# Splitting the next pair's keys ahead of a normalization, and another order of three products, in a fused attention and MLP kernel

## The chip, the cores and the metric

The kernel runs on one core of one Trainium2 chip. The time is the device time of one execution, in microseconds (us). Before the change it is 675.01 us, the median of three runs (674.80 to 675.87).

The engines by their names in the profile: PE is TensorE (matmuls) and PEld its loading of the stationary operand, DVE is VectorE, ACT is ScalarE, POOL is GpSimd, SP is SyncE, which here only issues DMAs. Each engine works through its own queue in order.

## The reference

Attention with a band of 96 keys and 8 global keys, then a two-layer MLP with a gate; 4 batches, 8 heads, 768 positions, 64 columns per head, 512 model columns, 2048 hidden ones. All is float32.

```python
scores = q @ k.T / sqrt(64) - slope[h] * dist       # where kept, else -1e9
a = exp(scores - max); a = a / (sum(a) + 1e-9)
x = (a @ v).reshape(3072, 512)
h = x @ w_in                                        # 512 -> 2048
g = h * clip(h + 3, 0, 6) / 6
out = g @ w_out                                     # 2048 -> 512
```

## The kernel before

**Numbers.** TensorE multiplies in a reduced float32 form (fp32r). To keep full precision each operand is split into a high and a low part, and a product is made of three: high times high, high times low, low times high. The parts of the hidden activation g are gh (made by GpSimd in the layers' part, L183, by ScalarE before it, L185) and gl = g - gh (VectorE, L190). The weights are w1h, w1l, w2h and w2l, decoded from their words while blocks 0 and 1 run (w2l by VectorE at L399). In the later attention queries are split into q1 (ScalarE, L751) and q2 (VectorE, L755), and keys into kx: the high part in one half of the partitions (GpSimd, L752), the low part in the other (VectorE, L758).

**Blocks and pairs.** The work is eight blocks of 384 positions (four batches, two halves each). Attention goes by pairs of heads, four pairs to a block, 32 pairs in all, numbered through. Pairs 0 to 11 (blocks 0 to 2) are done first, with plain float32 keys, beside the first halves of the MLP. Then comes *the layers' part*: while the MLP of block i runs (i from 2 on), the attention of block i + 1 is done beside it. So pairs 12 to 15 (block 3) are done beside the MLP of block 2, and pairs 16 to 31 beside the MLPs of blocks 3 to 6. Block 7's MLP runs alone.

**The MLP of a block.** It loops over f, 16 slices of 128 hidden columns. `first` (L159) makes hp, the hidden slice, with 12 matmuls of 384 columns. `gate` (L170) makes g on ScalarE and VectorE. gh and gl follow, and `second` (L193) adds the slice to three accumulators (three tiles tt of 128 positions) with nine matmuls of 512 columns, three per tile. `halves` (L438) puts `first` of f ahead of `second` of f - 1, so that the gate's chain runs beside TensorE's work. It yields after each `first` with its gate and after each `second`.

**Attention beside it.** `attention` (L586) fills a list of units for a block, six to a pair, and at each yield one unit's steps are put into the engines' queues. For a pair `me` and the next one, `after`, a pair's six units hold:

- units 0 to 2: `scores(t)` (L763), for each tile t of 128 queries four matmuls on kx with q1 and q2 (L778), the distances and the row minimum on VectorE (L785), the exponentials and their sums on ScalarE (L789);
- unit 3: `sum_up` (L793: add and reciprocal, L797 and L798), `normalize(0)` and `normalize(1)` (two multiplications each on GpSimd, L807), then `after.split(0)`: q1 and the high keys;
- unit 4: `normalize(2)`, `spread(0)`, and `after.split(1)`: q2;
- unit 5: `spread(1)`, `spread(2)`, `fetch`, and `after.split(2)`: the low keys, then the load of a pair further on.

`spread` (L822) transposes 32 x 32 blocks on VectorE (L832) and stores them to memory (L834); `fetch` (L837) reads them back as *weights* of the values (L841) with four DMAs. `values` (L850) multiplies them with v (L859). It is called for two pairs at once, in the sixth unit of every second pair. For pairs 12 to 15 all units come one place later, behind an empty one.

**What sets the order.** PE, GpSimd and SP keep the order of the program text as it runs (`in_order`, L576). VectorE and ScalarE are ordered by the framework's scheduler, which estimates times. So a step that is moved in a unit moves on GpSimd exactly so, and on VectorE as the scheduler sees fit. g has one buffer, gh, gl and hp two, the blocks that `spread` fills two.

Of the kernel before, what the change touches and what calls it, by code (L numbers as in the profile page):

```python
# [20 lines left out]
NT = 3  # L21
# [36 lines left out]
class Kernel:  # L58
# [134 lines left out]
    def second(self, f, acc, gh, gl):  # L193
        for tt in range(NT):
            tk = slice(tt * P, (tt + 1) * P)
            for j, (a, w) in enumerate(((gh, self.w2h), (gl, self.w2h), (gh, self.w2l))):
                self.nc.tensor.matmul(acc[tt], lhsT=a[:, tk], rhs=self.w2(w, f),  # L197
                                      start=(f == 0 and j == 0), stop=(f == NF - 1 and j == 2))

# [386 lines left out]
    def attention(self, i, x, first):  # L586

        units = [[] for _ in range(2 * NF - 2)]
        pairs = [first or Pair(self, i * NPAIR, x, False)]
        pairs[0].x = x  # L590
        if first is None:
            for k in range(3):
                pairs[0].split(k, False)
            units[1].append(lambda: self.load_next(pairs[0].n, False))
        for p in range(NPAIR):
            n = i * NPAIR + p
            me, after = pairs[p], Pair(self, n + 1, x, False) if n + 1 < len(self.blocks) * NPAIR else None
            pairs.append(after)
            at = units[6 * p:]
            for t in range(NT):  # L600
                at[t].append(lambda t=t, me=me: me.scores(t))
            at[3] += [me.sum_up, lambda me=me: me.normalize(0), lambda me=me: me.normalize(1)]
            at[4] += [lambda me=me: me.normalize(2), lambda me=me: me.spread(0)]
            at[5] += [lambda me=me: me.spread(1), lambda me=me: me.spread(2), me.fetch]
            for t in range(NT if after else 0):
                at[t + 3].append(lambda t=t, after=after: after.split(t))
            if p % 2 == 1:
                at[11] += [lambda me=pairs[p - 1]: me.values("x"), lambda me=me: me.values("s")]
        return units, pairs[NPAIR]
# [327 lines left out]
```

## Time and profile before

| What | us |
|---|---|
| median of three runs | 675.01 |
| the profiled execution | 674.91 |
| its span, first to last instruction | 673.0 |
| PE busy | 657.1 |
| VectorE busy | 438.6 |
| ScalarE busy | 282.9 |
| GpSimd busy | 192.6 |

The span is what the profile's rows lie in; 1.9 us of the execution lie around it. The granted TensorE clock is 0.998 of full speed. A row of a timeline gives the start in us from the span's start, how long the group took, engine and line, the operation, what it writes and reads, how many there are in the group, and in brackets how long the engine had stood idle before it and what ended that. Matmuls overlap, so a row's duration on PE is longer than the step from one matmul to the next: the steps are read from the starts. A row of the waits gives the total, the number of times and the longest.

### The profile page before, as it was taken

Reading aid. Unit: us, or ns where it says so; the run is one execution under the profiler, and the core shown is the slowest. Engines: PE = TensorE matmul, PEld = TensorE weight load, DVE = VectorE, ACT = ScalarE, POOL = GpSimd, SP = SyncE. Lnnn points to the kernel's source line nnn. Section 1 sums busy time; section 2 is a strip of 40 time slices with the busy share of each in tenths; the row PEclk is TensorE's granted clock in tenths of the full one; section 3 lists DMA queues with packets and bytes.
Section 4 is the critical chain, followed back from the end, with each engine's and each line's share of the span. In section 5 each row is a group of like instructions: output and inputs, shape, how many; then the busy total and the mean of one; then the engine's idle time right before and its main releaser. Section 6 shows DMA issues by size and latency. Waiting matters only on the chain.

```text
span 673.0 us, 11339 instructions
## 1 busy us (share of the span) xinstructions
PE 657.1 (98%) x3913; PEld 590.5 (88%) x3913; DVE 438.6 (65%) x1186; ACT 282.9 (42%) x744; POOL 192.6 (29%) x354
## 2 busy tenths in 40 slices
PE   7999899999999999999999999999999999999996
PEld 6788789999999889899989999899989999989995
DVE  8799899999975666457653676447762676422221
ACT  6899655554446333144333433143331443231111
POOL 2855400000000443233340343315431343302110
PEclk9999999999999999999999999999999999999999
DMA  8677432333303446524654367534555255510001
GB/s 255 176 230 242 146 124 100 121 110 110 97 29 133 131 135 181 158 94 132 165 140 119 103 172 189 147 94 126 138 160 141 79 150 142 141 47 2 1 1 52
DMA packets 62611, 84.33 MB, mean 125 GB/s; under 512 B 8784, under 2 KB 48720, under 8 KB 62544
## 3 DMA queue, kind: packets, MB, share of 16 engines
q1 hardware_dynamic: 62256, 83.25, 43.1%
q8 instruction: 33, 0.54, 0.3%
q14 instruction: 34, 0.28, 0.1%
q10 hardware_dynamic: 288, 0.26, 0.1%
HBM read 62.52 MB, written 20.97 MB: 124 GB/s over the span
## 4 chain that ended last, share of the span: by engine, by line
PE 84%; DMA 5%; ACT 4%; DVE 3%; issue 1%; POOL 1%; SPq 0%; POOLq 0%; ACTq 0%
PE hp L165 38%; PE acc L197 32%; DMA wst<-w 5%; ACT n L789 2%; PE sp L778 2%; PE xp L859 2%; PE tp L859 2%; PE sp L197 2%; PE tp L197 2%; PE xp L197 2%; PE tp L778 2%; POOL n L807 1%; ACT pt L819 1%; DVE n L785 1%; ACT wz L370 0%
## 5 line engine op out<-in xcount | busy, mean ns | idle before, releaser
L176 ACT ACTIVATE g<-hp,small 128x384 f32<-128x384 f32 x127 | 73.9, 582 | 256.0 <-PE hp L165 226.1
L165 PE MATMUL hp<-xh,w1h 128*128 128x384 f32 x512 | 174.0, 340 | 0.0
L165 PE MATMUL hp<-xh,w1l 128*128 128x384 f32 x512 | 172.8, 337 | 0.0
L165 PE MATMUL hp<-xl,w1h 128*128 128x384 f32 x512 | 171.9, 336 | 0.0
L183 POOL TENSOR_SCALAR gh<-g 128x384 fp32r<-128x384 f32 x96 | 57.8, 602 | 295.1 <-DVE g L177 265.2
L197 PE MATMUL acc<-w2h,gl 128*128 128x512 f32 x336 | 132.9, 396 | 0.1
L197 PE MATMUL acc<-w2l,gh 128*128 128x512 f32 x336 | 132.8, 395 | 0.0
L197 PE MATMUL acc<-w2h,gh 128*128 128x512 f32 x336 | 132.2, 393 | 0.0
L807 POOL TENSOR_SCALAR n<-n,sums 128x232 f32<-128x232 f32 (+1 forms) x186 | 104.9, 581 | 52.6 <-DVE sums L798 47.0
L177 DVE SCALAR_TENSOR_TENSOR g<-g,hp 128x384 f32<-128x384 f32 x128 | 70.2, 549 | 76.0 <-ACT g L176 75.4
L789 ACT ACTIVATE n<-n,least 128x232 f32<-128x232 f32 (+1 forms) x192 | 89.7, 471 | 40.3 <-DVE least L785 39.6
L190 DVE TENSOR_TENSOR gl<-g,gh 128x384 fp32r<-128x384 f32 x128 | 73.2, 572 | 45.7 <-POOL gh L183 44.0
L165 PEld LDWEIGHTS hp<-xh,w1h 128*128 128x128 f32 x512 | 96.3, 188 | 5.5 <-issue 1.5
L165 PEld LDWEIGHTS hp<-xl,w1h 128*128 128x128 f32 x512 | 96.2, 188 | 3.9
L165 PEld LDWEIGHTS hp<-xh,w1l 128*128 128x128 f32 x512 | 96.0, 188 | 0.0
L197 PEld LDWEIGHTS acc<-w2l,gh 128*128 128x128 f32 x336 | 63.0, 188 | 13.4
L197 PEld LDWEIGHTS acc<-w2h,gl 128*128 128x128 f32 x336 | 63.2, 188 | 11.8 <-DVE gl L190 1.5
L197 PEld LDWEIGHTS acc<-w2h,gh 128*128 128x128 f32 x336 | 63.3, 188 | 10.6 <-POOL gh L183 0.3
L832 DVE STREAM_TRANSPOSE blocks<-n 128x256 f32<-128x256 f32 x112 | 43.5, 424 | 27.1 <-POOL n L807 25.1
L752 POOL TENSOR_SCALAR kx<-load 64x504 fp32r<-64x504 f32 (+1 forms) x40 | 23.0, 575 | 119.0 <-PE hp L165 117.3
L785 DVE CUSTOM_DVE_ANT_0 n<-sp,d 128x232 f32<-128x232 f32 (+1 forms) x70 | 23.7, 376 | 36.8 <-PE sp L778 36.5
L789 ACT ACTIVATION_READ_ACCUMULATOR n<-n,least 128x1 f32 x192 | 36.9, 192 | 0.0
(113 smaller groups left out, 769.4 us busy)
## 6 DMA issues: line engine op xcount, KB each, us to landing
wst<-w SPq DMA_DIRECT2D x32, 512.0 KB, 3.5
there<-blocks SPq DMA_DIRECT2D x52, 256.0 KB, 2.6
load<-pairs SPq DMA_DIRECT2D x20, 636.0 KB, 5.2
load<-pairs SPq DMA_DIRECT2D x32, 384.0 KB, 4.0
weights<-there SPq DMA_DIRECT2D x48, 192.0 KB, 3.9
out<-o SPq DMA_DIRECT2D x23, 256.0 KB, 2.2
weights<-there SPq DMA_DIRECT2D x32, 160.0 KB, 3.3
load<-pairs SPq DMA_DIRECT2D x12, 252.0 KB, 4.7
```

The lines of the kernel that those rows point to most:

```text
L165: self.nc.tensor.matmul(hp, lhsT=self.w1(w, f)[:, kt, :], rhs=a[:, kt, :], start=(n == 0), stop=(n == 3 * NKT - 1))
L176: nc.scalar.activation(out=g, in_=hp, func=AF.Relu, bias=self.three, scale=1.0)
L177: nc.vector.scalar_tensor_tensor(out=g, in0=g, scalar=6.0, in1=hp, op0=ALU.min, op1=ALU.mult)
L183: self.nc.gpsimd.tensor_scalar(out=gh, in0=g, scalar1=1.0, scalar2=0.0, op0=ALU.mult, op1=ALU.add)
L190: self.nc.vector.tensor_tensor(out=gl, in0=g, in1=gh.bitcast(F32), op=ALU.subtract)
L197: self.nc.tensor.matmul(acc[tt], lhsT=a[:, tk], rhs=self.w2(w, f), start=(f == 0 and j == 0), stop=(f == NF - 1 and j == 2))
L778: nc.tensor.matmul(sp[:, j, lo:W], lhsT=q[:, t], rhs=part["kx"][:, c], start=(m == 0), stop=(m == 1))
L785: nc.vector.tensor_tensor_reduce(out=e[:, j, lo:W], in0=sp[:, j, lo:W], in1=d, op0=ALU.add, op1=ALU.min, scale=scale, scalar=3.0e38, accum ...
L789: nc.scalar.activation(out=e[:, j, lo:W], in_=e[:, j, lo:W], func=AF.Exp, bias=self.least[:, i:i + 1], scale=-1.0, accum_out=self.sums[:, ...
L807: nc.gpsimd.tensor_scalar(out=e[:, j, lo:W], in0=e[:, j, lo:W], scalar1=over, scalar2=0.0, op0=ALU.mult, op1=ALU.add)
L832: nc.vector.transpose(out=blocks[:, :, s].rearrange("p b j q -> p j b q"), in_=e[:, :, c:c + P].rearrange("p j (b q) -> p j b q", b=4))
L859: nc.tensor.matmul(xps[j * D:(j + 1) * D, t * P:(t + 1) * P], lhsT=vt[0:K, t, j * D:(j + 1) * D], rhs=self.part(t, j, c, K), start=(c == 0 ...
```

## The change

Two edits. The first takes `split(0)` of the next pair out of its place behind `normalize(0)` and `normalize(1)` and puts it at the head of unit 3, ahead of `sum_up`; `split(1)` and `split(2)` stay. The second changes the order of the three products of a tile in `second`: high-high, high-low, low-high, so that the product that reads gl comes last. It holds for all blocks.

```diff
     def second(self, f, acc, gh, gl):
         for tt in range(NT):
             tk = slice(tt * P, (tt + 1) * P)
-            for j, (a, w) in enumerate(((gh, self.w2h), (gl, self.w2h), (gh, self.w2l))):
+            for j, (a, w) in enumerate(((gh, self.w2h), (gh, self.w2l), (gl, self.w2h))):
                 self.nc.tensor.matmul(acc[tt], lhsT=a[:, tk], rhs=self.w2(w, f),
                                       start=(f == 0 and j == 0), stop=(f == NF - 1 and j == 2))
...
             for t in range(NT):
                 at[t].append(lambda t=t, me=me: me.scores(t))
+            if after:
+                at[3].append(lambda after=after: after.split(0))
             at[3] += [me.sum_up, lambda me=me: me.normalize(0), lambda me=me: me.normalize(1)]
             at[4] += [lambda me=me: me.normalize(2), lambda me=me: me.spread(0)]
             at[5] += [lambda me=me: me.spread(1), lambda me=me: me.spread(2), me.fetch]
-            for t in range(NT if after else 0):
+            for t in range(1, NT if after else 0):
                 at[t + 3].append(lambda t=t, after=after: after.split(t))
```

Lines from L602 on have a number higher by two after the change. The first place is GpSimd beside the MLP of block 2, while pair 12 is normalized and pair 13's keys are split. Before:

```order
L183 TENSOR_SCALAR gh<-g 128x384 x3
L807 TENSOR_SCALAR n<-n,sums 128x232 x4
L752 TENSOR_SCALAR kx<-load_73 64x504 x2
L807 TENSOR_SCALAR n<-n,sums 128x232 x2
L183 TENSOR_SCALAR gh<-g 128x384 x3
```

After:

```order
L183 TENSOR_SCALAR gh<-g 128x384 x3
L754 TENSOR_SCALAR kx<-load_73 64x504 x2
L809 TENSOR_SCALAR n<-n,sums 128x232 x6
L183 TENSOR_SCALAR gh<-g 128x384 x3
L754 TENSOR_SCALAR kx<-load_72 64x504 x2
```

The two high keys now stand ahead of all six normalizations, which follow each other without a break.

The second place is VectorE at the same time; `blocks` are the transposes of `spread`, four of them for tiles 0 and 1 and two for tile 2, and `n,least` with `least` is a score's reduction. Before:

```order
L177 SCALAR_TENSOR_TENSOR g<-g,hp 128x384
L190 TENSOR_TENSOR gl<-g,gh 128x384
L832 STREAM_TRANSPOSE blocks<-n 128x2x4x32 x4
L758 TENSOR_TENSOR kx<-load_73,kx 64x504
L177 SCALAR_TENSOR_TENSOR g<-g,hp 128x384
L758 TENSOR_TENSOR kx<-load_73,kx 64x504
L832 STREAM_TRANSPOSE blocks<-n 128x2x4x32 x2
L190 TENSOR_TENSOR gl<-g,gh 128x384
```

After:

```order
L177 SCALAR_TENSOR_TENSOR g<-g,hp 128x384
L190 TENSOR_TENSOR gl<-g,gh 128x384
L760 TENSOR_TENSOR kx<-load_73,kx 64x504 x2
L834 STREAM_TRANSPOSE blocks<-n 128x2x4x32 x2
L177 SCALAR_TENSOR_TENSOR g<-g,hp 128x384
L834 STREAM_TRANSPOSE blocks<-n 128x2x4x32 x2
L190 TENSOR_TENSOR gl<-g,gh 128x384
L787 ISA n,least<-tp,d_92 128x232
L787 ISA least 128x1
L787 ISA n,least<-tp,d_92 128x232
L787 ISA least 128x1
L834 STREAM_TRANSPOSE blocks<-n 128x2x4x32 x2
```

Both low keys moved ahead of the transposes, and tile 2's transposes moved behind gl and behind the first score reductions of the next pair. For pair 14 and pair 15 they moved behind gl too, with no score reduction ahead of them.

The third place is VectorE beside the MLP of a later block (3), between the scores of a pair and its transposes. Before:

```order
L190 TENSOR_TENSOR gl<-g,gh 128x384
L797 TENSOR_SCALAR sums<-sums 128x6
L798 RECIPROCAL sums<-sums 128x6
L832 STREAM_TRANSPOSE blocks<-n 128x2x4x32
L177 SCALAR_TENSOR_TENSOR g<-g,hp 128x384
L832 STREAM_TRANSPOSE blocks<-n 128x2x4x32 x2
L758 TENSOR_TENSOR kx<-load_72,kx 64x400 x2
L190 TENSOR_TENSOR gl<-g,gh 128x384
```

After:

```order
L190 TENSOR_TENSOR gl<-g,gh 128x384
L799 TENSOR_SCALAR sums<-sums 128x6
L760 TENSOR_TENSOR kx<-load_72,kx 64x400
L800 RECIPROCAL sums<-sums 128x6
L760 TENSOR_TENSOR kx<-load_72,kx 64x400
L834 STREAM_TRANSPOSE blocks<-n 128x2x4x32
L177 SCALAR_TENSOR_TENSOR g<-g,hp 128x384
L834 STREAM_TRANSPOSE blocks<-n 128x2x4x32 x2
L190 TENSOR_TENSOR gl<-g,gh 128x384
```

One low key part moved between the two steps of `sum_up`, the other right behind them; the transposes and gl no longer have the low keys ahead of them in this stretch's second half.

## The prediction

> **What bounds the kernel now.** I read the page first, then the waits, then the timelines of TensorE, GpSimd and VectorE at the places where TensorE waits. The page says how much there is to win at all:
>
> ```profile
> PE 657.1 (98%) x3913; PEld 590.5 (88%) x3913; DVE 438.6 (65%) x1186; ACT 282.9 (42%) x744; POOL 192.6 (29%) x354
> ```
>
> TensorE is busy for 657.1 of 673.0 us. The change removes no matmul and adds none, so it can only take out places where TensorE waits, 16 us in all. The view of the waits has two rows that bear on the edits (engine and line, what it waited for, us in total, times, longest):
>
> ```profile
> POOL n L807 <- DVE sums L798: 47.0, 23, 7.2
> PEld acc L197 <- DVE gl L190: 1.5, 5, 0.4
> ```
>
> TensorE's loads wait five times for the low part gl. The first row says that GpSimd idles ahead of its normalizations, which matters below. The waits for keys I found in TensorE's timeline (start, us, then the group). First an undisturbed score group:
>
> ```profile
> 215.36 0.60 PE L778 MATMUL sp<-kx,q 128*128 128x232 f32 x4
> 215.80 0.34 PE L165 MATMUL hp<-xh,w1h 128*128 128x384 f32 x1
> ```
>
> Then the two groups, a pair apart, in which it waits for keys, and I found no others:
>
> ```profile
> 224.19 0.40 PE L778 MATMUL tp<-kx,q 128*128 128x232 f32 x2
> 225.43 0.46 PE L778 MATMUL tp<-kx,q 128*128 128x232 f32 x2 [0.84 <-DVE kx L758]
> 225.72 0.35 PE L165 MATMUL hp<-xh,w1h 128*128 128x384 f32 x1
> ```
>
> ```profile
> 239.19 0.41 PE L778 MATMUL sp<-kx,q 128*128 128x232 f32 x2
> 240.44 0.46 PE L778 MATMUL sp<-kx,q 128*128 128x232 f32 x2 [0.84 <-DVE kx L758]
> ```
>
> Four score matmuls take 215.80 - 215.36 = 0.44 us from start to start; with the wait in them 225.72 - 224.19 = 1.53, so 1.09 lost. The second place loses (240.44 - 239.19) - 0.22 = 1.03 and then the same refill of about 0.07: 1.10. **Key waits: 2.19 us.**
>
> Who made the keys late? GpSimd and VectorE just ahead of the first place:
>
> ```profile
> 219.53 0.51 POOL L183 TENSOR_SCALAR gh<-g 128x384 fp32r<-128x384 f32 x1 [4.19 <-DVE g L177]
> 220.02 2.17 POOL L807 TENSOR_SCALAR n<-n,sums 128x232 f32<-128x232 f32 x4
> 222.16 1.30 POOL L752 TENSOR_SCALAR kx<-load 64x504 fp32r<-64x504 f32 x2
> 223.56 1.20 POOL L807 TENSOR_SCALAR n<-n,sums 128x232 f32<-128x232 f32 x2
> 224.74 0.92 POOL L183 TENSOR_SCALAR gh<-g 128x384 fp32r<-128x384 f32 x1
> ```
>
> ```profile
> 221.35 1.64 DVE L832 STREAM_TRANSPOSE blocks<-n 128x256 f32<-128x256 f32 x4 [0.72 <-POOL n L807]
> 223.02 0.96 DVE L758 TENSOR_TENSOR kx<-load,kx 64x504 fp32r<-64x504 f32 x1
> 224.02 0.56 DVE L177 SCALAR_TENSOR_TENSOR g<-g,hp 128x384 f32<-128x384 f32 x1
> 224.61 0.68 DVE L758 TENSOR_TENSOR kx<-load,kx 64x504 fp32r<-64x504 f32 x1
> 225.31 0.77 DVE L832 STREAM_TRANSPOSE blocks<-n 128x256 f32<-128x256 f32 x2
> 226.01 0.51 DVE L190 TENSOR_TENSOR gl<-g,gh 128x384 fp32r<-128x384 f32 x1
> ```
>
> The high keys wait on GpSimd behind four normalizations, the low keys on VectorE behind four transposes. The second low part ends at 224.61 + 0.68 = 225.29, and TensorE goes on at 225.43.
>
> **Edit 1, keys ahead of the normalization.** I replay the same durations in the new order. GpSimd: gh ends at 220.04; both high keys take 1.30, to 221.35; six normalizations take 2.17 + 1.20, to 224.7; gh takes 0.92, to 225.6. VectorE: both low keys are at most 0.96 each and cannot end before 221.35 + 0.96 = 222.3. TensorE asks for them from 224.19 on: 1.9 us of margin, and the queries' q2 stand where they stood. So both key waits go: -2.19. What is late next? gl: 225.6 + 0.51 = 226.1, against 226.52 before. The third pair of transposes: in this block VectorE now does them after gl and, for its first two pairs (12 and 13), after the next score reductions as well. TensorE waits for neither directly, but the transposes start the way through memory that brings the weights of the values back.
>
> ScalarE keeps its order. The DMA queue (SP) keeps its order too: the split that moved issues no DMA, only its third step does, and that stays.
>
> In blocks 4 to 7 the keys cost GpSimd nothing, because it was waiting there, as its row in one such pair shows:
>
> ```profile
> 420.01 1.77 POOL L807 TENSOR_SCALAR n<-n,sums 128x232 f32<-128x232 f32 x4 [1.35 <-DVE sums L798]
> ```
>
> Two keys, 1.30 us by the row above, go into 1.35 us of idle time. On VectorE one low part now stands ahead of the reciprocal, which puts the normalizations back by 0.7 to 1 us; but the keys' 1.30 is gone from behind them, so gh and gl come 0.3 to 0.6 sooner than now. No TensorE wait is made there; without that cover the keys would put gh 1.30 later, and TensorE, which waits for gl in five places now, has no margin for that.
>
> **The new cost: pair 15.** The last pair of block 3 must have its weights back from memory early. The queue's rows and TensorE's use of them (the single line is the landing of those four fetches, minimum, median, maximum):
>
> ```profile
> 269.07 4.08 SPq L834 DMA_DIRECT2D there<-blocks  x3
> 277.09 1.73 SPq L841 DMA_DIRECT2D weights<-there  x4
> ```
>
> ```profile
> DMA to landing us min/median/max: 2.9/3.7/4.3
> ```
>
> ```profile
> 283.05 1.49 PE L859 MATMUL tp<-weights,load 128*64 128x128 f32 x24
> ```
>
> The last of the four fetches is issued at about 277.09 + 3/4 of 1.73 = 278.4 and lands 4.3 later at the most, 282.7: a margin of 0.35 us. With the new order the third transposes follow gl; by the replay above that is 226.1 + 0.8 = 226.9 instead of 226.08, so 0.85 later. If all else takes as long, TensorE waits 0.85 - 0.35 = 0.5 us. But the last store before the fetch, issued when the transposes ended (about 272.6), let it go at 277.09 only, 4.5 us on, and the page has less for a store:
>
> ```profile
> there<-blocks SPq DMA_DIRECT2D x52, 256.0 KB, 2.6
> ```
>
> At 2.6 there is no wait at all. I take 0.25, between ends of 0 and 0.5. Pair 13 has the same way to go, with more room now:
>
> ```profile
> 243.80 1.80 SPq L841 DMA_DIRECT2D weights<-there  x4
> ```
>
> ```profile
> DMA to landing us min/median/max: 2.9/4.2/5.4
> ```
>
> ```profile
> 253.60 1.49 PE L859 MATMUL tp<-weights,load 128*64 128x128 f32 x24
> ```
>
> Its last fetch, at 245.2, lands by 250.6, 3.0 us ahead. 2.2 of that go when TensorE comes sooner by the two key waits, and some 0.3 with the later transposes (they stand behind the reductions, but all work before them is 1.1 earlier by then). It should just pass.
>
> **Edit 2, the order of the products.** gl is asked for one matmul later, at the third place of a group. TensorE at one of the five waits for it, and at the last one of the program:
>
> ```profile
> 346.81 0.40 PE L197 MATMUL acc<-w2h,gh 128*128 128x512 f32 x1
> ```
>
> ```profile
> 347.69 0.40 PE L197 MATMUL acc<-w2h,gh 128*128 128x512 f32 x1
> ```
>
> ```profile
> 665.33 0.51 PE L197 MATMUL acc<-w2h,gh 128*128 128x512 f32 x1
> 665.92 0.49 PE L197 MATMUL acc<-w2h,gl 128*128 128x512 f32 x1
> 666.26 0.39 PE L197 MATMUL acc<-w2l,gh 128*128 128x512 f32 x1
> 666.49 0.40 PE L197 MATMUL acc<-w2h,gh 128*128 128x512 f32 x1
> ```
>
> An undisturbed step is 666.49 - 666.26 = 0.23. At 346.81 three steps take 0.88 instead of 0.69: 0.19 lost, less than a step, so it goes whole. At the end three steps take 1.16. gl is ready no sooner there, so after the change two products run ahead of it instead of one and just one step, 0.23, is won. The other three share what the row of the waits leaves, 1.5 - 0.4 for the longest and less for this one; a load that waits is partly covered by the matmul before it, as here, so I take 0.15 each. **Edit 2: 0.19 + 0.23 + 0.45 = 0.9 us**, from 0.4 (the two shown) to 1.3 (the row's 1.5, with 0.23 for the 0.4 at the end). The low weights w2l are now needed a step, 0.23, sooner. They are made on VectorE while blocks 0 and 1 run; the nearest call is the fifth:
>
> ```profile
> 89.02 0.68 DVE L399 TENSOR_TENSOR w2l<-we,w2h 128x512 fp32r<-128x512 f32 x1
> ```
>
> ```profile
> 95.31 0.40 PE L197 MATMUL acc<-w2l,gh 128*128 128x512 f32 x1
> ```
>
> They are there 5.6 us ahead, so nothing new waits.
>
> Its other effect is that the same stationary operand is loaded twice in a row. The first layer has this already:
>
> ```profile
> L165 PEld LDWEIGHTS hp<-xl,w1h 128*128 128x128 f32 x512 | 96.2, 188 | 3.9
> ```
>
> w1h stands twice in a row there, first for xh, then for xl (L164), yet this second load is made all 512 times. I cost the repeat at nothing. The Trainium skill, "TensorE: Matmul & The Clock Gate", section "Step-by-step: what each phase is for", says that weights are loaded apart so that one load can serve many matmuls. This row shows no load spared; what sparing them would give is rival 4.
>
> **The sum.** 2.19 + 0.9 - 0.25 = 2.84 us off. The profiled execution took 674.91 us, 1.9 more than its span, and stands 0.1 below the median of 675.01. So its span becomes 670.2, its time 672.1, the median 672.2.
>
> **Rivals.**
> 1. *The products' order does all.* The keys are made on GpSimd sooner, but TensorE still waits for them, because their low parts sit on VectorE behind gl, the gate and whatever the scheduler puts there. Against it: 1.9 us of margin. Then 0.9 is left: 674.1.
> 2. *Two engines in each other's way.* In the rows above gh takes 0.51 alone and 0.92 beside a low key part. The new order puts both low parts beside normalizations, and each may hold GpSimd up by up to 0.57 to 0.96. Then the third transposes come another 0.6 to 1.2 later, and pair 15's wait becomes 1.1 to 1.7: the gain is 3.1 - 1.5 = 1.6, the time 673.4. The Trainium skill, "SBUF — State Buffer", section "SBUF: two separate sides", says that a VectorE operation with two SBUF inputs and a GpSimd operation lock each other out for a whole instruction; by that rule it would come out this way, and the 0.92 agrees.
> 3. *Slower: the weights come back too late.* The path store, fetch, landing is slow by turns: in pair 15 the store took 4.4. If it takes 2 us longer, and a fetch another 2, pair 15 waits 0.5 + 4 = 4.5 us, and the time is 675.0 - 3.1 + 4.5 = 676.4. It decides from the point where the wait exceeds 3.1. For it: 0.35 us of margin. Against it: pair 13, next in line, has 3.0 before the change.
> 4. *A repeated stationary operand is cheaper.* The chain has twelve 384-column steps of the first layer in one piece:
>
> ```profile
> 652.92 2.10 PE hp L165 x12
> ```
>
> That is 0.175 each; 0.230 for 512 columns leaves about 0.01 per matmul that doesn't grow with the columns. 384 repeats (16 values of f, 3 tiles, 8 blocks) would give 3.8 more: 668.4. The 512 loads above speak against it.
>
> **How the numbers follow.** The forecast, 0.64. Rival 1, 0.11; rival 2, 0.15; rival 3, 0.06; rival 4, 0.04. A measurement of this kernel can tell about 0.2%, 1.35 us, from no change: faster means below 673.66. The forecast, rival 4 and nearly all of rival 2 are faster: 0.64 + 0.04 + 0.13 = 0.81; rival 1 and the rest of rival 2 the same: 0.13; rival 3, with its point of decision just short of the bound, 0.06 slower. The forecast's own ends are 2.19 + 1.3 = 3.5 (671.5) and 2.19 + 0.4 - 0.5 = 2.1 (672.9). The range goes on to rivals 1 and 2, 674.1, and below to 671.2 for the run's own spread (674.80 to 675.87 before).
>
> **What would show it.** Right: no TensorE wait for kx in the view of waits; the high keys directly behind gh on GpSimd; waits for gl at most at the end, about 0.1; a values group of pair 15 with a wait for weights below 0.5; TensorE's matmul steps still 0.175 and 0.23. Wrong: a wait for kx in either place (rival 1), a long wait of the values' matmuls for a fetch (rivals 2 and 3), or steps in the second layer below 0.23 (rival 4).

## The result, and the profile after

The kernel after the change takes 671.61 us (median of 5 runs, 671.16 to 672.71), the kernel before 675.87 (5 runs, 674.80 to 677.79). The ratio is 0.9945, with a 95% interval of 0.9927 to 0.9963: 2.5 to 4.9 us faster. The forecast was 2.84 faster, 672.2.

The profiled execution took 671.61, its span is 669.7, and TensorE is still all but full. The first row is the page's, the second the only row in the view of waits in which TensorE waits for gl, and in no row does it wait for kx (kernel after):

```profile
PE 655.5 (98%) x3913; PEld 590.1 (88%) x3913; DVE 444.0 (66%) x1186; ACT 282.4 (42%) x744; POOL 195.6 (29%) x354
PEld acc L197 <- DVE gl L190: 0.8, 3, 0.3
```

Between two spans the edit is not the only difference, so I cut the span at two marks of TensorE: the `second` that starts near 204 us, just ahead of the layers' part, and the end of the last matmul. These are the first and last matmul of that stretch, before and then after:

```profile
203.83 0.40 PE L197 MATMUL acc<-w2h,gh 128*128 128x512 f32 x1
667.65 0.39 PE L197 MATMUL acc<-w2l,gh 128*128 128x512 f32 x1
```

```profile
203.12 0.39 PE L197 MATMUL acc<-w2h,gh 128*128 128x512 f32 x1
663.97 0.39 PE L197 MATMUL acc<-w2h,gl 128*128 128x512 f32 x1
```

Before, the stretch lasts 667.65 + 0.39 - 203.83 = 464.2; after, 461.2. **The layers' part is 2.96 shorter.** The stretch ahead of it is 0.7 shorter by chance: in ten profiles of this study it ended anywhere from 203.1 to 204.5, and a second profile of the same kernel after ended it at 203.85. Behind the last matmul 0.4 was lost again: 5.4 to the end of the span, against 5.0.

TensorE at the two places where it waited for keys (after):

```profile
223.28 0.61 PE L780 MATMUL tp<-kx,q 128*128 128x232 f32 x4
223.72 0.34 PE L165 MATMUL hp<-xh,w1h 128*128 128x384 f32 x1
...
237.18 0.61 PE L780 MATMUL sp<-kx,q 128*128 128x232 f32 x4
237.62 0.34 PE L165 MATMUL hp<-xh,w1h 128*128 128x384 f32 x1
```

Four score matmuls take 0.44 from start to start in both, as in the undisturbed group before. What made it so, on GpSimd and then VectorE (after, the first of the two places):

```profile
218.62 0.51 POOL L183 TENSOR_SCALAR gh<-g 128x384 fp32r<-128x384 f32 x1 [4.20 <-DVE g L177]
219.09 1.49 POOL L754 TENSOR_SCALAR kx<-load 64x504 fp32r<-64x504 f32 x2
220.68 3.37 POOL L809 TENSOR_SCALAR n<-n,sums 128x232 f32<-128x232 f32 x6
```

```profile
219.16 0.94 DVE L190 TENSOR_TENSOR gl<-g,gh 128x384 fp32r<-128x384 f32 x1 [0.73 <-POOL gh L183]
220.14 1.83 DVE L760 TENSOR_TENSOR kx<-load,kx 64x504 fp32r<-64x504 f32 x2
```

The high keys stand directly behind gh. The low keys end at 220.14 + 1.83 = 221.97, 1.3 us ahead of TensorE's 223.28. That is less than the 1.9 of the forecast, mostly since gl took 0.94 beside the keys on GpSimd instead of 0.51.

Pair 15, the forecast's new cost: the queue's rows, the landing of its last store, then TensorE's values (after):

```profile
267.44 3.92 SPq L836 DMA_DIRECT2D there<-blocks  x3
273.42 1.73 SPq L843 DMA_DIRECT2D weights<-there  x4
```

```profile
DMA to landing us min/median/max: 2.6/2.6/2.6
```

```profile
279.92 1.49 PE L861 MATMUL tp<-weights,load 128*64 128x128 f32 x24
```

There is no wait. The last fetch landed at 279.32 by the trace, 0.60 ahead; before, the margin was 0.36. Not all of such a margin is free: in e5 and e6 below, where TensorE does wait for this landing, its first matmul starts 0.24 and 0.25 behind it.

### The profile page after: what moved, and what is told of

The parts are those of the page before. It is cut to its first block, busy times and chain, and to the rows that moved or that the text cites. A ratio compares the mean times of both kernels' runs of the same rounds, so it can differ in the third digit from the quotient of the medians.

```text
span 669.7 us, 11388 instructions
## 1 busy us (share of the span) xinstructions
PE 655.5 (98%) x3913; PEld 590.1 (88%) x3913; DVE 444.0 (66%) x1186; ACT 282.4 (42%) x744; POOL 195.6 (29%) x354
## 4 chain that ended last, share of the span: by engine, by line
PE 89%; ACT 4%; DMA 3%; DVE 1%; POOL 1%; issue 1%; SPq 0%
PE hp L165 39%; PE acc L197 34%; DMA wst<-w 3%; PE xp L861 3%; PE sp L780 2%; ACT n L791 2%; PE tp L861 2%; PE sp L197 2%; PE tp L197 2%; PE xp L197 2%; PE tp L780 2%; ACT pt L821 1%; PE acc L776 1%; POOL n L809 0%; SPq L296 0%
## 5 line engine op out<-in xcount | busy, mean ns | idle before, releaser
L183 POOL TENSOR_SCALAR gh<-g 128x384 fp32r<-128x384 f32 x96 | 51.7, 538 | 293.4 <-DVE g L177 262.5
L190 DVE TENSOR_TENSOR gl<-g,gh 128x384 fp32r<-128x384 f32 x128 | 78.1, 610 | 46.9 <-POOL gh L183 45.5
L197 PEld LDWEIGHTS acc<-w2h,gh 128*128 128x128 f32 x336 | 63.3, 188 | 10.4 <-POOL gh L183 0.3
L197 PEld LDWEIGHTS acc<-w2l,gh 128*128 128x128 f32 x336 | 63.2, 188 | 10.4
L754 POOL TENSOR_SCALAR kx<-load 64x504 fp32r<-64x504 f32 (+1 forms) x40 | 30.8, 770 | 118.8 <-PE hp L165 117.2
```

What stands on the lines that cost most here:

```text
L183: self.nc.gpsimd.tensor_scalar(out=gh, in0=g, scalar1=1.0, scalar2=0.0, op0=ALU.mult, op1=ALU.add)
L190: self.nc.vector.tensor_tensor(out=gl, in0=g, in1=gh.bitcast(F32), op=ALU.subtract)
L754: nc.gpsimd.tensor_scalar(out=part["kx"][own, c], in0=k[own, c], scalar1=1.0, scalar2=0.0, op0=ALU.mult, op1=ALU.add)
```

## The experiments

Each was timed beside the kernel before on the same chip: the first four on one, where the kernel before had a median of 675.54 (23 runs), the others on a second, where it had 675.81 (17 runs). "Layers' part" is the stretch between the two marks above, in the profiled execution; it is 464.20 before and 461.24 after.

| Kernel | median, us (runs) | ratio to before, 95% | layers' part |
|---|---|---|---|
| e1 keys only | 673.17 (5) | 0.9966, 0.9953 to 0.9979 | 462.11 |
| e2 order only | 674.45 (11) | 0.9983, 0.9974 to 0.9993 | 463.19 |
| e3 keys moved in block 3 only | 672.88 (5) | 0.9958, 0.9945 to 0.9971 | 461.01 |
| e4 keys moved in later blocks only | 675.46 (12) | 0.9998, 0.9988 to 1.0008 | 464.09 |
| e5 keys on ScalarE | 671.60 (5) | 0.9942, 0.9926 to 0.9957 | 461.75 |
| e6 pair 15's store later | 675.12 (11) | 0.9994, 0.9978 to 1.0009 | 463.16 |
| e7 the same in the kernel before | 675.60 (1) | - | 464.13 |
| e8 the kernel after again | 672.05 (6) | 0.9946, 0.9930 to 0.9962 | 461.29 |

**One edit each (e1, e2).** e1 has only the keys moved (the cuts of code are against the kernel after):

```diff
-            for j, (a, w) in enumerate(((gh, self.w2h), (gh, self.w2l), (gl, self.w2h))):
+            for j, (a, w) in enumerate(((gh, self.w2h), (gl, self.w2h), (gh, self.w2l))):
```

> Edit 1 alone, the products in the old order. Theory: the gain of edit 1 is the two waits for keys in block 3's pairs, 2.2 us, and nothing else; in later blocks gl comes later against TensorE with the keys moved (0.4 us at the place near 391 us of the changed kernel's trace, where gl ended 0.39 after its group's first matmul), so with gl asked for at the second place two new waits of about 0.3 each appear (near 391 and 547), while those near 347 and 503 go (0.36). Sum 1.9 us faster than the kernel before, no wait for kx on TensorE, four or five waits for gl. Rival (the prediction's words): gl comes sooner in later blocks, then all waits for gl but the last two go and it is 2.6 us faster.

e2 has only the new order of the products, with `split` left where it was:

```diff
-            if after:
-                at[3].append(lambda after=after: after.split(0))
...
-            for t in range(1, NT if after else 0):
+            for t in range(NT if after else 0):
```

> Edit 2 alone, the keys in their old place. Theory: 0.9 us faster than the kernel before, from five waits for gl (0.20, 0.19, 0.09, 0.17 go whole, 0.23 of the last); both waits for kx of 1.0 stay in the profile; steps of the second layer stay at 0.23. Rival (a repeated stationary operand is cheaper): steps fall below 0.23 and it gains more than 2 us. Rival (edit 2 does nothing by itself): 0.

In the layers' part e1 gains 2.09 and e2 1.01; together 3.10, and both edits at once gain 2.96. The interval of e1's median, 1.4 to 3.2 us, holds its theory and its rival, so the time can't decide between them; e2's, 0.5 to 1.8, excludes both of its rivals. The waits of e2, then of e1:

```profile
PE tp L778 <- DVE kx L758: 0.8, 1, 0.8
PE sp L778 <- DVE kx L758: 0.8, 1, 0.8
PEld acc L197 <- DVE gl L190: 0.3, 1, 0.3
```

```profile
PEld acc L197 <- DVE gl L190: 1.9, 6, 0.5
```

e2 leaves both key waits as they were and takes four of five waits for gl, all but the last. e1 takes the key waits. Its row for gl is longer than the 1.5 in 5 of before, but one of the six, 0.5 at 161.72 us, stands ahead of the layers' part. In it there are five as before, of 1.5 us, though not the same five. Compared matmul by matmul with the kernel before, the two that cost 0.19 and 0.17 near 347 and 503 us are gone, and two new ones have come. The first of these, beside the MLP of a later block (e1):

```profile
391.76 0.39 PE L197 MATMUL acc<-w2h,gh 128*128 128x512 f32 x1
392.12 0.50 PE L197 MATMUL acc<-w2h,gl 128*128 128x512 f32 x1
392.45 0.40 PE L197 MATMUL acc<-w2l,gh 128*128 128x512 f32 x1
```

Two steps take 0.69 instead of 0.46, and near 548 us 0.22 is lost in the same way. So in the later blocks the moved keys take 0.36 of waits and make 0.45, where the prediction had them make none.

**The keys moved in one part of the blocks (e3, e4).** Both have the new order of the products. e3 moves the keys only beside block 2's MLP, where block 3's attention is done; e4 (with `i != 3`) only in the later blocks.

```diff
-            if after:
+            if after and i == 3:
                 at[3].append(lambda after=after: after.split(0))
...
-            for t in range(1, NT if after else 0):
+            for t in range(1 if i == 3 else 0, NT if after else 0):
```

> Both edits, but the keys are moved for the pairs of block 3 alone (13 to 16), not in later blocks. Theory: the whole gain of edit 1 lies in these pairs, so this is as fast as the changed kernel or up to 0.2 faster, 3.1 us faster than the kernel before; no wait for kx; no wait for gl near 391 and 547. Rival (later blocks gain too, by gh and gl coming sooner): slower than the changed kernel by 0.5 or more.

> Both edits, but the keys are moved in the later blocks alone, not for block 3. Theory: no gain from edit 1 there; both waits for kx of 1.0 stay, gl waits near 391 and 547 as in the changed kernel, so 0.75 us faster than the kernel before, 2.3 slower than the changed kernel. Rival (later blocks gain too): 1.3 or more faster than the kernel before.

e3 against e2 gains 463.19 - 461.01 = 2.18, all that the keys were to bring. e4 against e2 loses 0.90 where nothing was expected, and gains 0.11 on the kernel before instead of 0.75 (its interval ends at 0.8): the key waits stayed as the theory has it, but its size failed in the layers' part. The waits of e4, then of e3:

```profile
PEld acc L197 <- DVE gl L190: 1.1, 4, 0.3
PE sp L780 <- DVE kx L760: 0.8, 1, 0.8
PE tp L780 <- DVE kx L760: 0.8, 1, 0.8
```

```profile
PEld acc L197 <- DVE gl L190: 0.5, 2, 0.3
```

In the full change the same loss is smaller: its layers' part is 0.23 to 0.28 longer than e3's, with 0.08 and 0.09 of it in the two places near 391 and 547 us. Compared matmul by matmul with e2, 0.62 of e4's 0.90 stands in one place, near 550 us, and 0.10 near 536. In e4's trace a gh on GpSimd starts at 535.25, 0.46 behind the end of the g that it reads, where the same one in the change starts 0.16 behind it. In the 10 us ahead of it VectorE and GpSimd run alike to 0.01 us in both; behind it they run 0.3, then 0.7 later than in the change, and TensorE waits for gh at 550.36. What held that one gh back stays open. The medians can't part e3 from the change (0.9958 and 0.9945, intervals overlapping).

**What makes gl late there (e5).** VectorE in one later pair, before:

```profile
388.24 0.55 DVE L190 TENSOR_TENSOR gl<-g,gh 128x384 fp32r<-128x384 f32 x1
388.71 0.16 DVE L797 TENSOR_SCALAR sums<-sums 128x6 f32<-128x6 f32 x1
388.90 0.19 DVE L798 RECIPROCAL sums<-sums 128x6 f32<-128x6 f32 x1
...
393.77 0.70 DVE L190 TENSOR_TENSOR gl<-g,gh 128x384 fp32r<-128x384 f32 x1
```

The same pair after, VectorE, then GpSimd and TensorE:

```profile
385.15 0.95 DVE L190 TENSOR_TENSOR gl<-g,gh 128x384 fp32r<-128x384 f32 x1
386.03 0.58 DVE L799 TENSOR_SCALAR sums<-sums 128x6 f32<-128x6 f32 x1
386.64 0.68 DVE L760 TENSOR_TENSOR kx<-load,kx 64x504 fp32r<-64x504 f32 x1
387.35 0.19 DVE L800 RECIPROCAL sums<-sums 128x6 f32<-128x6 f32 x1
...
390.98 0.56 DVE L190 TENSOR_TENSOR gl<-g,gh 128x384 fp32r<-128x384 f32 x1
```

```profile
384.80 1.79 POOL L754 TENSOR_SCALAR kx<-load 64x504 fp32r<-64x504 f32 x2
387.74 2.16 POOL L809 TENSOR_SCALAR n<-n,sums 128x232 f32<-128x232 f32 x4 [1.16 <-DVE sums L800]
```

```profile
391.15 0.40 PE L197 MATMUL acc<-w2h,gh 128*128 128x512 f32 x1
...
391.62 0.47 PE L197 MATMUL acc<-w2h,gl 128*128 128x512 f32 x1
391.93 0.39 PE L197 MATMUL acc<-w2h,gh 128*128 128x512 f32 x1
```

While GpSimd makes keys (384.80 to 386.59), gl takes 0.95 instead of 0.55 and a sum of six columns 0.58 instead of 0.16. The sum, started at 386.03, ended with the keys: 386.61 against 386.59. With the low key ahead of the reciprocal, the normalizations still stand 1.16 idle before they start. The second gl ends at 391.54, 0.39 behind the start of its group; before, it ended at 394.47, 0.03 ahead of it (394.50). Only because the product that reads gl now comes third does TensorE lose no more than 391.93 - 391.62 - 0.23 = 0.08.

Is it the two engines beside each other, or the order? e5 makes the high keys on ScalarE, and so takes the work off GpSimd, while both low keys stay ahead of the reciprocal:

```diff
-                nc.gpsimd.tensor_scalar(out=part["kx"][own, c], in0=k[own, c], scalar1=1.0, scalar2=0.0,
-                                        op0=ALU.mult, op1=ALU.add)
+                nc.scalar.copy(out=part["kx"][own, c], in_=k[own, c])
```

> The changed kernel, with the high keys copied by ScalarE and not by GpSimd. In the later blocks of the changed kernel gl at 385.15 took 0.95 us beside GpSimd's keys, where it took 0.55 before the change, and a six-column sum of sum_up took 0.58. Theory: VectorE and GpSimd hold each other up there. Then gl in that place takes about 0.56 again, the sum about 0.16, and TensorE's waits for gl near 391 and 547 us go; that is 0.2 to 0.5 us in all, so the time is 671.2 to 671.6, and the view of waits has at most the one for gl at the end of the program, 0.3. Rival: gl is late because a low key stands ahead of the reciprocal, so it is the order and not the sharing; then the same waits stay (3 of 0.8 us in all) and the time is as after, 671.6. A third way: ScalarE, with two more copies ahead of the gate's work, makes g later, and new waits for gl come, 0.5 us or more.

VectorE and TensorE in the same pair (e5):

```profile
387.18 0.55 DVE L190 TENSOR_TENSOR gl<-g,gh 128x384 fp32r<-128x384 f32 x1
387.76 0.68 DVE L759 TENSOR_TENSOR kx<-load,kx 64x504 fp32r<-64x504 f32 x1
388.47 0.17 DVE L798 TENSOR_SCALAR sums<-sums 128x6 f32<-128x6 f32 x1
```

```profile
392.96 0.40 PE L197 MATMUL acc<-w2l,gh 128*128 128x512 f32 x1
393.19 0.39 PE L197 MATMUL acc<-w2h,gl 128*128 128x512 f32 x1
393.42 0.39 PE L197 MATMUL acc<-w2h,gh 128*128 128x512 f32 x1
```

gl and the sum are back at 0.55 and 0.17, the steps at 0.23, and the waits near 391 and 547 us are gone. The scheduler even put both low keys ahead of the sum here, so the order alone doesn't make the wait; the keys on GpSimd do, by their length and by the way they slow VectorE. These two parts weren't tried apart. The median, 671.60, stands at the upper end of the theory's 671.2 to 671.6, and beside the 672.05 of the change in the same set (e8) it decides nothing. The layers' part is 0.5 longer than in the change. Two new waits for gl came near 241 and 271 us (with the last one 0.7 in 3, where the theory had one), but they cost 0.05 by the matmuls' starts; the loss is pair 15's, as below.

**How near pair 15 was (e6, e7, e8).** e6 does the transposes of pair 15's third tile four times over in the kernel after, e7 twice in the kernel before:

```diff
-            nc.vector.transpose(out=blocks[:, :, s].rearrange("p b j q -> p j b q"),
-                                in_=e[:, :, c:c + P].rearrange("p j (b q) -> p j b q", b=4))
+            for _ in range(4 if self.n == 15 and t == 2 else 1):
+                nc.vector.transpose(out=blocks[:, :, s].rearrange("p b j q -> p j b q"),
+                                    in_=e[:, :, c:c + P].rearrange("p j (b q) -> p j b q", b=4))
```

> The changed kernel, with each of the transposes of pair 15's third tile done four times over (repeated work, the same values), so that the last store of this pair starts some 2.4 to 3.3 us later. It tells what rival 3 of the prediction would have cost. Theory: the way from the store to the weights is 0.60 us early in the changed kernel, and all lateness beyond that is paid one for one: TensorE waits 1.8 to 2.7 us ahead of pair 15's values, and the time is 673.4 to 674.3, still not slower than before. Rival: the later store meets other transfers or other cover, so that less than half of the lateness is paid (wait under 1.2, time under 672.8), or the queue behind it shifts too and a later pair pays as well (over 3.1, time over 674.7).

TensorE's values of pair 14 and pair 15 (e6):

```profile
279.92 1.54 PE L862 MATMUL xp<-weights,load 128*64 128x128 f32 x24
283.21 1.54 PE L862 MATMUL tp<-weights,load 128*64 128x128 f32 x24 [1.75 <-DMA weights<-there]
```

The step between them is 3.29 instead of the 279.92 - 278.55 = 1.37 of the kernel after: 1.92 lost, and the layers' part is 1.92 longer (463.16 against 461.24), so nothing else pays and nothing is covered. The last store was issued 2.39 later, counted from the first mark. Less the margin of 0.60, with the 0.25 from the landing to the first matmul, and less 0.13 by which the last fetch took shorter, that is 1.91: one for one, as expected. The median rose by 3.1 (675.12 against e8's 672.05, each uncertain by about 1 us). That lies outside the theory's times and in the rival's, though the wait is not the rival's; the 1.2 that the trace doesn't show stays open. It is no slower than before.

> The kernel before, with each of the transposes of pair 15's third tile done twice (repeated work, the same values), so that the store starts about 0.8 us later, as the change was expected to make it. Before, that store took 4.4 us until the fetch could go, with a 16 KB packet of the instruction queue in the midst of it; after the change it took 2.6. Theory: 4.4 is a matter of what else the queues carry at that moment; moved by 0.8 us the store lands in about 2.6 to 3, the fetch goes no later than before and TensorE does not wait for pair 15's weights. Rival: the store takes 4.4 for another reason; then the fetch goes 0.8 later and TensorE waits about 0.4 us ahead of these values.

The queue, the store's landing and the values (e7):

```profile
268.99 5.21 SPq L835 DMA_DIRECT2D there<-blocks  x3
276.88 1.73 SPq L842 DMA_DIRECT2D weights<-there  x4
```

```profile
DMA to landing us min/median/max: 3.2/3.2/3.2
```

```profile
282.97 1.49 PE L860 MATMUL tp<-weights,load 128*64 128x128 f32 x24
```

The store started 1.0 later than before, took 3.2 instead of 4.4, and the fetch went at 276.88, no later than before (277.09); no wait. It is the theory's outcome, though the store took a little longer than the theory's 2.6 to 3. Pair 15's last store in all ten profiles, with the one 16 KB packet of the page's "q8 instruction" queue that passes near it (times by the trace's packets, from the store's issue):

```
kernel   packet starts, after the issue   store lands, after the issue
after    -0.24                            2.55
e3       -0.09                            2.56
e1       +0.01                            2.56
e8       +0.15                            2.58
e7       +0.47                            3.18
e2       +2.28                            4.34
e4       +2.28                            4.37
before   +2.28                            4.43
e5       +2.30                            4.35
e6       -2.52                            2.56
```

The packet takes 0.88 to 1.16. Before, three of the store's 528 packets moved only behind that packet's end, at 3.2 to 3.4 us; in the kernel after the last one ended at 2.2. So the 4.4 was a packet of instructions in the way. The packets seem to be TensorE's own: from the fifth to the 31st of the program they come on average 253 of its matmuls and loads apart (200 to 296), and this one, the 13th, falls behind 3167 of them in the kernel after and 3177 in the kernel before, while the steps counted in VectorE's instructions go from 10 to 53. What moves it by a microsecond or two stays open.

e5 shows the price. The packet fell late again, and pair 15's values come late (e5):

```profile
279.46 1.54 PE L860 MATMUL xp<-weights,load 128*64 128x128 f32 x24
281.43 1.54 PE L860 MATMUL tp<-weights,load 128*64 128x128 f32 x24 [0.43 <-DMA weights<-there]
```

1.97 instead of 1.37: 0.6 of its layers' part.

> The changed kernel as it is, beside the three others and the kernel before on one chip. Theory: 671.6, within 0.6; in the trace the layers' part takes 461.2 us again, no wait for keys, and waits for gl of 0.8 us in all at the same three places; the stretch ahead of the layers' part and the one behind TensorE's last matmul may differ by some tenths from run to run. Rival: part of the 3.4 us was the run's luck, and the gain is nearer the forecast's 2.8 (672.2) or less.

e8 confirms the part in the layers (461.29) and the three waits of 0.8 for gl; with 0.9946 the gain is 2.6 to 4.7 us.

## Why the prediction was right, and where it was not

**Key waits, 2.19: right.** They are gone, and e3 against e2 gives 2.18 for them. Rival 1 is dead: the low keys were 1.3 us early.

**Edit 2, 0.9: right.** e2 gives 1.01 in the layers' part and about 1.1 in the medians. At the end two products run ahead of gl and one step was won, as worked out; four of the five waits went. TensorE's steps stayed at 0.23, so rival 4 is dead: a repeated stationary operand is loaded again here as in the first layer.

**"In blocks 4 to 7 ... gh and gl come 0.3 to 0.6 sooner than now. No TensorE wait is made there": wrong.** Near 391 us gl came 0.4 us later against TensorE, and the waits for gl that are left, 0.8 in 3, miss the prediction's own sign of being right (at most at the end, about 0.1). The step counted the keys' 1.30 as free because GpSimd stood idle, and didn't count what they do to VectorE meanwhile. The keys took 1.79 there, gl 0.95 and the sum 0.58. e1 shows the two waits that this made, 0.45 in all. In two other pairs the step held, and the 0.36 of waits near 347 and 503 us went. Edit 2 hides most of the new ones: of the 0.45, 0.17 is left in the full change. This is also why e1 and e2 don't add up: both count the 0.36 near 347 and 503, and 0.28 is hidden, so 3.10 becomes 3.10 - 0.36 + 0.28 = 3.0, against 2.96.

**Pair 15, 0.25: near the measured 0 by luck, since errors cancel.** Counted from the first mark, TensorE came 2.42 sooner, and the third transposes 1.08 sooner only: 1.34 later against TensorE, where the forecast had 0.85. It had them follow gl, but they waited longer (VectorE, after):

```profile
268.88 0.56 DVE L190 TENSOR_TENSOR gl<-g,gh 128x384 fp32r<-128x384 f32 x1 [0.35 <-POOL gh L183]
270.05 0.77 DVE L834 STREAM_TRANSPOSE blocks<-n 128x256 f32<-128x256 f32 x2 [0.61 <-DMA there<-blocks]
```

gl ended at 269.44, and right behind it the transposes would have been 0.74 later against TensorE, near the replay's 0.85. But `blocks` has two buffers, and the first tile's store, issued at 267.44, landed only 2.59 later, at 270.03. Before, it had landed at 271.64, 0.19 ahead of the third transposes. The prediction put this wait at nothing. Over the program, the view of waits has VectorE idle for 10.4 us until such stores landed, against 1.5 before. Rival 2's mechanism adds at most a part, by high keys that took 1.32 there instead of 1.13 and so made the first store later.

The fetch's landing took another 0.30. Against that the store took 2.55 instead of 4.43. The margin is 0.36 - 1.34 - 0.30 + 1.88 = 0.60, of which 0.35 was free, since 0.25 goes from the landing to the first matmul; in the same way only 0.1 of the forecast's 0.35 was. With the store of before TensorE would have waited 1.28 + 0.25 = 1.5 us, an estimate, and the gain in the layers' part would have been 2.96 - 1.5 = 1.4, just below rival 2's 1.6. The prediction saw that 2.6 was possible; that the packet would fall elsewhere it could not see.

Rival 2's mechanism, two engines in each other's way, is shown by e5, and the Trainium skill, "SBUF — State Buffer", section "SBUF: two separate sides", has it as a lock between GpSimd and a VectorE operation that has two SBUF inputs or runs in a two-port mode; for gl, which has two inputs, the 0.95 beside GpSimd and the 0.55 without agree. The sum has one input, and whether it ran in such a mode no run here shows, but it was slowed too, from 0.16 to 0.58.

**Rival 3, slower:** e6 made the store 2.4 later and lost 1.9. Beyond its margin the path pays one for one, as the rival said, and its point of decision (a wait over 3.1) wasn't reached.

**Pair 13** "should just pass": its margin fell from 3.04 to 1.43 us by the trace.

**The sum.** 2.84 was forecast, the layers' part gave 2.96 and 2.91 in two profiles. The rest of the difference of the medians, 4.26 and 3.76, is in no wait that the profiles show; both intervals reach down to 2.6 or less. For the first, 0.86 of it lies in the kernel before: its median was 675.01 in three runs and 675.87 with two more.

## What to carry to other kernels

Idle time on an engine is not free room: work put there can slow a second engine beside it, so check what the neighbour does in that stretch, and how long its operations take beside such work elsewhere in the trace. Count, too, when a step's output buffer comes free: work that comes sooner can run into the store that still reads the buffer. Where a moved operand arrives late by less than a step or two, using it last in its group hides the lateness. To size a gain of half a percent, cut the span at fixed instructions of the bounding engine: the stretch between them repeated to 0.05 us here, while its start moved by 1.4.

## What the runs showed of the hardware

- One 16 KB packet of the instruction queue made a 256 KB store land after 4.4 us instead of 2.6 when it fell 2.3 us behind the store's issue. It cost 0.6 when it fell 0.47 behind it, and nothing when it fell up to 0.15 behind it or ahead of it. Where it falls differs between kernels that differ only in the order of some instructions. The packets come every 253 TensorE instructions on average.
- VectorE's sum of 128x6 with one input took 0.58 beside GpSimd's keys, against 0.16 to 0.17 without them. Over the whole program gl took 610 ns on average with the keys moved, 572 before, and 559 with the keys on ScalarE.
- Where TensorE waited for a fetch, its first matmul started 0.24 (e5) and 0.25 (e6) us behind the landing.
- With two buffers, the transposes into the first one again waited until its store had landed, 2.6 us behind its issue: 0.61 us idle in pair 15 of the kernel after.
